# Gated-loop attention with a squared-ReLU block: the first unit's last pair of heads computed with steps on partitions and transposed on TensorE

## The chip, the cores and the metric

The kernel runs on one core of a Trainium2 chip. The metric is device time in microseconds. Three runs of the kernel before gave 648.28, 649.67 and 650.78; the median is 649.67.

## The reference

```
# q, k, v, a_re, a_im: (4, 8, 768, 48); w_in: (384, 2048); w_out: (2048, 384); all float32
mag = sqrt(a_re**2 + a_im**2)
scale = minimum(mag, 0.999) / (mag + 1e-6)
ar, ai = a_re * scale, a_im * scale
for t in range(768):                       # S_re, S_im: (4, 8, 48, 48), zero at the start
    S_re, S_im = ar_t * S_re - ai_t * S_im + outer(k_t, v_t),  ar_t * S_im + ai_t * S_re
    y_t = q_t @ S_re
x = y, heads side by side                  # (3072, 384)
out = maximum(x @ w_in, 0)**2 @ w_out      # (3072, 384)
```

So each head carries a complex state through 768 steps, and its rows of y, put side by side, go through two dense products.

## The kernel before

The 3072 rows are worked off in six units of 512 steps (NU = 6, L = 512), each in four chunks j of C = 128 steps (W = 4). The eight heads go in four pairs (NP = 4). The attention of a unit ends in xT, the transposed input of the dense part: xT[128 rows, unit % 2, m, 512 steps], where m is one of three blocks of 128 model columns. Pair i fills model columns 96 i to 96 i + 95: pair 0 and the first third of pair 1 lie in m=0, the rest of pair 1 and 64 columns of pair 2 in m=1, and the last 32 columns of pair 2 and all of pair 3 in m=2.

For a pair, these steps follow each other (lines of the kernel before):

- turn_pe transposes the scaled q and k on TensorE (L1660) and ACT copies them to QT (L1664).
- score makes the products of q and k (L1681, into bank sc0 or sc1, here sc_115 and sc_116), and DVE multiplies them by the causal mask into A (L1684).
- keep makes the chunk's contributions to the state (L1730, into tr_117 or tr_118), which ACT (L1740) or DVE (L1744) adds up in St and S.
- mix makes y of the pair: for unit 0, two products for each chunk and head, A with v (L1769) and the rotated q with the state St (L1773). The product's rows are the head's dimensions, two heads at partitions 0 to 47 and 64 to 111 of one bank. ACT copies the bank to the buffer yt (L1784), and DMAs bring its rows to their place in xT (L1797).

Unit 0's last pair (pair 3, heads 6 and 7) is done in two halves of 256 steps (by_half), the first in bank yp, the second in tr_118; its DMAs go half on SP's queue and half on ACT's. In the tables of order below, yt_94 and yt_95 are the two buffers yt (pair 2 has yt_94, pairs 1 and 3 yt_95), d_112 to d_114 the banks of the dense part, w_66 is the converted w_in and w_67 a buffer of w_out; aq_69 and f_70 belong to unit 1's inputs.

The dense part (function dense) multiplies w1 with xT (L1830, three matmuls for each block of 128 hidden columns and 256 steps, one for each m), applies ReLU and the square (L1863, L1864), and multiplies by w2 (L1878, or L1941 and L2086 in later units). For the first group of unit 0, six blocks have their m=0 and m=1 matmuls as twelve single steps ahead of everything else ("early" steps); the m=2 matmul of these blocks comes as a step of its own ("late").

On POOL, a small copy from xT's last rows of m=2 (the gate, L2179) stands ahead of the conversion and the fetches of later pieces of w_out. The conversion of the weights into the two-part form in which TensorE multiplies them (L978 to L992) runs on ACT and DVE between all this.

The order of the instructions on every engine is written out: the table ORDER gives for each engine a list of step numbers, and each engine's queue is filled in that order. SP and ACT issue DMAs in the same order.

Of the kernel before, what the change touches and what calls it, by code (L numbers as in the profile page):

```python
# [481 lines left out]
class Plan:  # L482
# [12 lines left out]
            220-222 2 0-1 5 4 224 3 6 225 223 226 14 7 13 15 9 17 16 8 228 19 12 11 18 10 20 227  # L495
            229 22 230 21 23-25 237 236 234 231 238 235 233 232 26-27 239-240 28 243 30-31 29 242
            241 35 49 33-34 42 32 48 46 45 47 43 244 44 246 245 40 36 38-39 37 41 51 50 55 57 54
            53 59 52 58 56 66 63 68 248 65 67 69 64 247 62 74 76 73 75 78 80 77 79 250 249 85 90
            60 84 89 87 91 88 86 61 72 71 70 81 83 82 93 92 252 254 253 251 99 95 101 94 98 96-97
            110 100 107 105 104 257 106 109 255 258 108 256 111 121 116 119-120 117-118 122 115  # L500
            261 260 262 259 132 130 133 131 129 103 127 126 128 102 112 123 114 113 124 135 125
            134 268 265 267 269 263-264 266 270 137-138 136 141 140 142 146 143 149 153 139 148
            152 272 150 271 147 151 160 159 162 157 163 161 164 158 273-274 173 171 169 175 174
            145 154 168 172 156 170 155 144 165 167 166 176-177 278 276 275 277 180 178 185 183
            182 181 184 192 194 190 179 188 193 189 191 195 204 206 202 205 201 200 203 199 186
            211 214 213 217 212 216 215 210 198 187 196-197 207 209 208 219 218 281 280 282 279
            283-285
        """,
        "POOL": """
            74-75 78 173 72 79 174 184 76 156 175 80 122 77 181 139 179 178 182 177 73 176 180 183  # L510
            9 8 10-11 13 12 14-15 89 185-186 189 188 187 82 17 91 83 81 84 191 86 85 90 95 0 19-20
            1 190 193 18 22 92 94 21 192 26 24 93 195 23 16 2 96 25 3 97 194 102 104 98 100 105 99
            103 101 27 109 108 28 30-31 34 29 33 112 32 41-42 87 107 111 38 106 37 36 110 39 35
            113 40 118 198 114 201 121 120 116 200 196 199 115 119 117 197 123 126 45 43-44 55 48
            127 46-47 125 129 52 51 53 128 130 124 50 88 54 49 137 134 132 204-205 4 133 5 203 138
            131 207 202 136 206 135 140 59 56 143 58 142 147 57 60 62-63 61 146 6 145 144 141 7
            213 152 211 155 148 154 149 210 151 150 212 153 159 208 64 164 67 65 160 66 209 68 158
            157 162 161 71 69-70 163 214 216 218 215 217 220 222 219 221 171 170 165 224 167 223
            172 169 168 226 225 227 166 230 228-229
        """,  # L520
        "PE": """
            539-553 0-1 554 2-3 555-559 4-6 560 7 561-565 8 566-570 42 571-574 44-45 43 48 53 51
            46-47 54 52 57 50 56 62 60 55 61 63 49 66 59 64 58 65 69-72 75 68 73 67 74 76 152
            77-79 154 160 155 161 153 162-163 158 166 156 164 159 165 167 172 157 174 173 168 178
            169 179 176-177 175 196 180 197 170 188 171 189-190 181-182 202-203 191 183 192
            184-185 193-194 186 195 187 200-201 198-199 206-207 204-205 212-213 210 208 80-81 209
            82 214 83 9 84-85 10 211 88 87 220 89-90 221 215 86 11-12 91-92 216 95 94 217 97 96
            222 98 14 13 99 218 223-225 93 15 102 101 100 219 226-227 103 16 228 232 229 231 233
            230 238-239 242 244 234-237 240 243 245 241 246-252 254 253 255-265 268-269 266-267
            270-273 17 105 104 276-278 274 279 275 106-107 18 108 281 280 282-284 111 110 109  # L530
            19-20 286 285 287-290 113-114 112 291-292 115 293-294 296 295 299 297-298 301-302 300
            303-304 307-308 305-306 309-312 314 313 315-316 319 317-318 320-321 323 322 324-326
            331-332 327-328 337 329-330 333 338 335-336 334 21 116-117 339-340 343 341-342 22 118
            23 120 119 345 344 347 346 25 123 122 121 24 349 348 350-352 26-27 124 126 125 355 353
            28 127 354 356-357 359 358 362-364 360-361 365 368 366-367 369-370 372 374 373 371 375
            377 376 378-382 386 383-385 387-391 394-396 392-393 400 397-398 401 399 29 128-129 402
            404 403 405 130 31 30 131-132 406-407 409 408 410 32-33 134-135 133 34 412 411 413 416
            414-415 136 35-36 138 137 418 417 139 419 422 420-421 427 423 425 428 424 426 433
            429-432 435-436 434 437-445 447 446 448-449 451-452 450 453-454 457 455 458-459 456
            463 460 464 461-462 465 469 466-468 38 140 37 141 471 473 143 142 39 144 470 472 475  # L540
            474 145 40 146-147 476 479 477 480 478 150 149 148 481 151 482 486 485 483 490 484 488
            487 492 489 491 496 493 498 497 494-495 499-500 505 501-502 506 503-504 509 508 511
            507 512 510 513 515 514 516-519 521 520 522-527 529 41 528 531 530 532-538
        """,
        "DVE": """
            363-364 367-368 365 371 366 372 369-370 375 377 376 378 373 381-382 374 383 379 384
            380 386 393 385 394 387 395-396 388 397-398 390 399-400 389 401-402 391 403-404 392
            510-511 405-426 428 427 429-430 432 431 433-434 436 435 437-440 442 441 443 486 444
            472 446 449-451 474 461 452 473 475 462-463 477 453 445 464 476 487-488 455 454 489
            456 447-448 457-458 478 459 465 491 466 490 467 460 468-470 480 479 471 481 186 492  # L550
            187 482 184-185 483 512 494 493 484 191 485 495 522 192 496-497 189-190 498 188 513
            499 519-520 194 196 500 197 195 514-515 193 521 523 198-201 524 202 526 525 516 528
            517-518 532 501 527 534 502 203 530 529 506 503 507 535 531 504 546-547 505 533 508
            548 509 549 558-559 550 560-561 551 562 552 563 553 564 555 565 554 566-567 556-557
            568-569 536 570-571 537 572 540 573-577 538 578 539 579-580 541 581-592 542 593 543
            594-595 544 596-598 545 600 599 601-602 607 604 608 603 609 605 610 606 617-618 615
            643 611 629-630 616 645 657 644 620 631 619 658-659 646 621 632 648 634 633 623 622
            647 624 660 625 635 626-628 636 661-662 637 649 638-639 612 640-642 206 663 651 650
            207 613-614 652 205 204 653 665 654 664 666 655 667-668 656 669-670 743 216 211 217
            210 208 224 209 744 218 745 749 228 750 746 671-672 212 673-674 213 676 675 747 677  # L560
            748 214 751 678 752 220 683-684 219 685 221 686 215 688 687 679 689-691 680 692 682
            681 694 693 696 695 697-705 223 706-715 225 716-717 227 718 226 719-724 229 725-729
            230 730-731 733 732 735 739 734 738 736 740 737 0 741 795 767 755 769 756 753-754 768
            1 757-758 3 2 4 770 797 742 772 7 759 5 9 6 8 771 783 761 773 760 762 10 763-764 796
            765 12 11 774 13 775 784 776 766 777-779 14 780 231-233 798 800 799 781-782 786 785
            239-240 801 241 787 803 802 804 236 805-806 235 234 237 788 238 789 222 790-791 807
            792-794 808 247-249 255 242 881 15 244 243 18 256-257 16 245 17 882 19 246 883 21 20
            251 22 887-888 250 809 260 24 261 23 884 810 252 811-813 253 814 262 815-816 254 885
            25 886 259 258 889 27 26 890 28 821-824 826 825 29 827-829 817-818 830 819 832 831 820
            833-855 30 856-870 876 871 891 877 872 878 873 892 874 879 875 894-896 33 897 31 898  # L570
            908 32 36 34 880 899 37 909 35 39 900 38 910-911 901 40 902 42 903 43 41 904-907 44
            263-265 913 912 271 914 272-273 916 915 917-918 266-267 919-921 45 279 268 280 269 46
            281 988 287-289 274 48 276-277 893 49 275 47 270 989 52 990 283 50 994 282 995 51 922
# [155 lines left out]
def fast_path(ctx, tc, q, k, v, a_re, a_im, moe_w_in, moe_w_out, out, flag):  # L729
# [874 lines left out]
    def pairs(n, which):  # L1604
# [197 lines left out]
        def by_half(i):  # L1802
            return n == 0 and i == NP - 1
# [447 lines left out]
```

## Time and profile before

| | |
|---|---|
| median of three runs | 649.67 us (648.28 to 650.78) |
| the profiled execution | 650.27 us |
| its span, first to last instruction | 648.1 us |
| mean granted TensorE clock | 0.985 |
| instructions | 12935 |

A row of a timeline reads: start in us, duration in us, engine, line, operation, output<-inputs, shape, and how many instructions are in it; brackets give the idle time ahead of it and what ended it. Durations of matmuls in a row overlap, because they are pipelined; the distance of starts tells the rate. A matmul in float32 shows as two passes ("x2"). The windows' rows give for each stretch the busy time of each engine; the chain is the work that ended last, followed back from the end. Starts are counted from the span's begin.

### The profile page before, as it was taken

The numbers are of one execution on the slowest core, as the hardware profiler recorded it, in microseconds if no ns is written. First come the engines' busy times: TensorE is split into PE (matmuls) and PEld (weight loads), VectorE is DVE, ScalarE is ACT, GpSimd is POOL, SyncE is SP. The second block draws the span as 40 slices with busy tenths as digits, with TensorE's granted clock in tenths as the row PEclk, the third lists the DMA queues.
The fourth block names the chain that finished last, engine by engine and source line by source line (L and its number), as shares of the span: only waits on it lengthen the run. The fifth ranks groups of instructions, "written<-read, shape, count | busy, mean of one in ns | idle before, by whom it ended". The sixth has DMA issues, their size and how long they took to land.

```text
span 648.1 us, 12935 instructions
## 1 busy us (share of the span) xinstructions
PE 603.7 (93%) x4762; PEld 539.9 (83%) x4762; DVE 581.9 (90%) x1192; ACT 378.9 (58%) x760; POOL 149.7 (23%) x266
## 2 busy tenths in 40 slices
PE   0448999999999999999999999999999999999995
PEld 0337987687778989999989999989989989988995
DVE  7999999999999999999988999988999998479981
ACT  7269998788868547536556636466545553432530
POOL 7401110145130034032123041113031042025200
PEclk9968999999999999999999999999999999999999
DMA  6973585026640057452076563066350064369721
GB/s 220 336 222 82 120 226 162 8 58 166 166 108 13 6 108 181 123 146 52 7 156 157 115 143 61 13 165 166 86 144 23 16 144 112 80 217 299 252 74 31
DMA packets 55913, 80.42 MB, mean 124 GB/s; under 512 B 12032, under 2 KB 38400, under 8 KB 55840
## 3 DMA queue, kind: packets, MB, share of 16 engines
q0 software_dynamic: 16064, 42.12, 23.6%
q1 hardware_dynamic: 35168, 31.93, 19.8%
q10 hardware_dynamic: 4608, 5.44, 3.2%
q8 instruction: 40, 0.66, 0.5%
q14 instruction: 33, 0.27, 0.1%
HBM read 48.76 MB, written 4.72 MB: 83 GB/s over the span
## 4 chain that ended last, share of the span: by engine, by line
PE 86%; DVE 6%; DMA 2%; ACT 1%; issue 1%; SPq 1%; ACTq 0%; DVEq 0%
PE d L1830 30%; PE d L1941 27%; PE d L1878 6%; PE sc L1681 5%; PE tr L1730 3%; PE yp L1762 3%; PE d L2086 2%; PE yp L1765 2%; PE tr L2086 2%; PE sc L1830 2%; PE sc L2086 1%; DMA xT<-yt 1%; PE d L1660 1%; DVE f L1150 1%; PE tr L1660 1%; PE yp L2086 1%
## 5 line engine op out<-in xcount | busy, mean ns | idle before, releaser
L1830 PE MATMUL d<-xT,w 128*128 128x256 f32 x888 | 197.9, 380 | 1.0 <-DMA xT<-yt 1.0
L1830 PEld LDWEIGHTS d<-xT,w 128*128 128x128 f32 x888 | 167.7, 190 | 25.1 <-issue 2.0
L1941 PE MATMUL d<-T,g 128*128 128x192 f32 x576 | 100.6, 328 | 0.3 <-DVE g L1957 0.3
L1941 PEld LDWEIGHTS d<-T,g 128*128 128x128 f32 x576 | 94.0, 190 | 1.5 <-DVE g L1957 0.6
L1896 POOL DMA_DIRECT2D out_dram<-ot x80 | 48.5, 610 | 157.8 <-DVE ot L1966 140.0
L1863 ACT ACTIVATE g<-d 128x512 f32<-128x512 f32 x74 | 43.7, 591 | 63.0 <-PE d L1830 55.3
L1941 PE MATMUL d<-w,g 128*128 128x192 f32 x432 | 76.7, 328 | 0.0
L1941 PEld LDWEIGHTS d<-w,g 128*128 128x128 f32 x432 | 71.0, 190 | 1.3 <-ACT g L1864 0.2
L1582 POOL DMA_DIRECT2D KC<-f x60 | 36.0, 604 | 127.5 <-DVE f L1545 120.0
L1864 ACT ACTIVATE g<-g 128x512 f32<-128x512 f32 x80 | 50.5, 631 | 2.5
L1957 DVE TENSOR_TENSOR g<-g 128x512 f32<-128x512 f32 x72 | 48.4, 682 | 3.9 <-PE d L1941 3.6
L1480 DVE TENSOR_TENSOR f<-aq,xn 128x384 f32<-128x384 f32 (+1 forms) x72 | 45.9, 682 | 0.0
L1634 DVE STREAM_TRANSPOSE aq<-f 128x384 f32<-128x384 f32 (+1 forms) x51 | 44.0, 910 | 0.2
L1878 PE MATMUL d<-w,g 128*128 128x384 f32 x128 | 43.7, 489 | 0.0
L1681 PE MATMUL sc<-QT 96*64 96x64 f32 (+1 forms) x736 | 38.6, 250 | 0.0
L1150 DVE TENSOR_TENSOR f<-aq 128x384 f32<-128x384 f32 x72 | 36.8, 550 | 0.2
L1681 PEld LDWEIGHTS sc<-QT 96*64 96x64 f32 x736 | 35.1, 137 | 2.0 <-issue 1.4
L1966 DVE TENSOR_TENSOR ot<-ot,d 128x192 f32<-128x192 f32 x70 | 23.6, 347 | 14.4 <-PE d L1941 14.0
L1878 PEld LDWEIGHTS d<-w,g 128*128 128x128 f32 x128 | 23.7, 190 | 14.0
L1073 POOL DMA_DIRECT2D v<-in_v_dram x30 | 23.3, 778 | 34.4 <-ACT junk L1452 25.7
L1511 ACT ACTIVATE f<-aq 128x768 f32<-128x768 f32 (+1 forms) x16 | 17.3, 1080 | 14.9 <-DVE aq L1497 14.9
L1730 PEld LDWEIGHTS tr<-v,KC 128*33 128x33 f32 (+1 forms) x544 | 19.2, 126 | 4.3 <-issue 3.4
(329 smaller groups left out, 1169.4 us busy)
## 6 DMA issues: line engine op xcount, KB each, us to landing
QT<-aq SPq DMA_DIRECT2D x136, 64.0 KB, 2.2
f<-in_moe_w_in_dram POOLq DMA_DIRECT2D x8, 768.0 KB, 6.7
f<-in_moe_w_out_dram POOLq DMA_DIRECT2D x8, 768.0 KB, 5.1
QT<-aq ACTq DMA_DIRECT2D x68, 64.0 KB, 2.2
KC<-f POOLq DMA_DIRECT2D x40, 96.0 KB, 3.1
out_dram<-ot POOLq DMA_DIRECT2D x80, 48.0 KB, 3.6
xT<-yt SPq DMA_DIRECT2D x34, 96.0 KB, 2.3
T<-in_moe_w_out_dram POOLq DMA_DIRECT2D x4, 768.0 KB, 7.8
```

Of the source, the lines that this page charges most:

```text
L1150: lambda c=c, j=j: dve.tensor_tensor(out=f[:, j], in0=a[:, :, :, c - 1], in1=a[:, j, :, c].unsqueeze(1).to_broadcast([C, 2, HH, D]), op=AL ...
L1480: lambda j=j, r=r: dve.tensor_tensor(out=f4[:, j, r], in0=a[:, r], in1=over(j), op=ALU.mult), rk)
L1634: lambda src=src, dst=dst: dve.transpose(out=dst, in_=src), rank)
L1681: pe.matmul(sa[p0:p0 + CH, j, t0:], lhsT=T[:, j, 1, h, t0:t0 + CH], rhs=T[:, j, 0, h, t0:], start=True, stop=True)
L1830: pe.matmul(ps, lhsT=w1[:, f // FP, m, ts(f % FP, C)], rhs=xT[:, n % 2, m, ts(grp, G)], start=(m == 0), stop=(m == NM - 1))
L1863: act.activation(out=o, in_=ps, func=AF.Relu)
L1864: act.activation(out=o, in_=o, func=AF.Square)
L1878: pe.matmul(ps, lhsT=gt[:, f % 2, ts(i, C)], rhs=w2[:, f], start=(f == 0), stop=(f == NF - 1))
L1896: dma(pool, [("ot", o, 0), ("ot", o, 1)], [], lambda p0=p0: pool.dma_start(out=out[r + p0:r + p0 + QC, :].rearrange("(t c) e -> c t e", c= ...
L1941: pe.matmul(bank[b][:, 0:DH], lhsT=gsets[x][h][:, j - HW * h, r], rhs=w(j), start=first and j == 0, stop=last and j == NT - 1)
L1957: lambda: dve.tensor_tensor(out=g[:, :, o], in0=g[:, :, x0], in1=g[:, :, x1], op=op),
L2086: pe.matmul(ps[:, jj], lhsT=u[:, ts(jj, C)], rhs=v_, start=i == 0, stop=i == len(terms) - 1)
```

## The change

In unit 0, pair 3 is computed the other way round. The product's rows are now the 128 steps of a chunk and its columns the 48 dimensions of a head (A and QT are the weights, v and the state the moving side). ACT copies a half (two chunks, two heads) to yt, whose first 32 columns of each chunk POOL has set to zero; TensorE transposes each chunk of 128 x 128 into a free part of the same bank; and ACT (upper 64 rows) and DVE (32 rows) copy that to xT. The two copies and four DMAs of before go. A key x5 stands for the part of xT that DVE writes. The table ORDER is replaced as a whole, on all five engines; of it only the effects shown below are told. Line numbers behind this place are 41 higher, those of the score and the state 3 higher: L1830 becomes L1871, L1684 L1687, L1744 L1747, L1797 L1838.

```diff
     def xk(n, ms, gs=(0, 1)):
-        return [("xT", n % 2, m, g) for m in ms for g in gs]
+        return ([("xT", n % 2, m, g) for m in ms for g in gs]
+                + [("x5", g) for m in ms for g in gs if n == 0 and m == NM - 1])
...
             y = take("yt", 2)
+            if by_half(i):
+                lead = C - 2 * D
+                step("POOL", 0.4, [], [("yt", y, 0), ("yt", y, 1)], lambda: pool.memset(
+                    yts[y].rearrange("p (j c) -> p j c", c=C)[:, :, 0:lead], 0.0), rank)
             for js, gs in ((range(2), [0]), (range(2, W), [1])) if by_half(i) else ((range(W), [0, 1]),):
...
+                if by_half(i):
+                    flat = bank[b][:, 0:len(js) * 2 * D].rearrange("p (j h d) -> p j h d", h=2, d=D)
+                    side = bank[b][:, L - C * len(js):L]
+                    def steps_first(js=js, flat=flat):
+                        for j in js:
+                            for h in range(2):
+                                o = flat[:, j - js[0], h]
+                                pe.matmul(o, lhsT=aa[h][:, j], rhs=v5[:, j, 2 * i + h],
+                                          start=True, stop=at[j] is None)
+                                if at[j] is not None:
+                                    pe.matmul(o, lhsT=T[:, j, 0, h], rhs=at[j][:, h],
+                                              start=False, stop=True)
+                    def as_rows(js=js, side=side):
+                        for q, j in enumerate(js):
+                            pe.transpose(side[:, ts(q, C)], yts[y][:, ts(j, C)], ident)
...
+                    step("PE", 0.45 * len(js), ..., [(b,)], steps_first, rank)
+                    step("ACT", ..., act.copy(
+                             out=yts[y][:, cols].rearrange("p (j c) -> p j c", c=C)[:, :, lead:],
+                             in_=flat.rearrange("p j h d -> p j (h d)")), rank)
+                    step("PE", 0.11 * len(js), yg, [(b,)], as_rows, rank)
+                    step("ACT", ..., act.copy(
+                             out=xT[64:C, n % 2, NM - 1, cols], in_=side[64:C]), rank)
+                    step("DVE", ..., dve.tensor_copy(
+                             out=xT[lead:64, n % 2, NM - 1, cols], in_=side[lead:64]), rank)
+                    continue
```

TensorE, from the end of pair 3's product to the dense stream (a row of 128x256 without a count is one early or late step). Before:

```order
L1769 MATMUL tr_118<-A_91,v_78 48x128
L1773 MATMUL tr_118<-QT_75,St_93 48x128 x2
L1830 MATMUL d_114<-xT,w_66 128x256
L1830 MATMUL sc_116<-xT,w_66 128x256
L1830 MATMUL d_114<-xT,w_66 128x256
L1830 MATMUL sc_116<-xT,w_66 128x256
L1830 MATMUL d_113<-xT,w_66 128x256
L1830 MATMUL yp<-xT,w_66 128x256 x2
L1830 MATMUL sc_115<-xT,w_66 128x256
L1830 MATMUL d_114<-xT,w_66 128x256
L1830 MATMUL d_112<-xT,w_66 128x256
```

The first two of these steps read m=0, and the third row of 128x256 (d_114's second) is the first that reads m=1; the next d_114 after sc_115 is the first late one, on m=2. One early step stood ahead of the product. After:

```order
L1773 MATMUL tr_118<-v_78,A_91 128x48
L1776 MATMUL tr_118<-St_93,QT_75 128x48
L1871 MATMUL sc_115<-xT,w_66 128x256
L1871 MATMUL d_114<-xT,w_66 128x256
L1871 MATMUL sc_116<-xT,w_66 128x256
L1781 MATMUL yp<-ident,yt_95 128x128 x2
L1781 MATMUL tr_118<-ident,yt_95 128x128 x2
L1871 MATMUL d_112<-xT,w_66 128x256
L1871 MATMUL sc_116<-xT,w_66 128x256 x5
L1871 MATMUL d_112<-xT,w_66 128x256
```

Three early steps now stand ahead of the product, three between it and the transposes, and two (d_112 and the first of sc_116's five) between these and the first late step, which is the second of the five.

DVE, from the masks of pair 3 on. Before:

```order
L992 ISA w_66<-w_67,w_66 128x1536 x2
L1744 TENSOR_TENSOR S_89<-tr_118,St_92 96x96
L1684 TENSOR_TENSOR A_90<-sc_115,mask 128x512
L1684 TENSOR_TENSOR A_91<-sc_116,mask 128x512
L1744 TENSOR_TENSOR St_93<-tr_118,St_93 96x96
L985 TENSOR_SCALAR w_66<-w_67 128x768
L1744 TENSOR_TENSOR St_93<-tr_118,St_93 96x96
L985 TENSOR_SCALAR w_66<-xT 128x768
```

After:

```order
L1687 TENSOR_TENSOR A_91<-sc_116,mask 128x512
L988 TENSOR_SCALAR w_66<-w_67 128x768
L1747 TENSOR_TENSOR St_93<-tr_118,St_93 96x96
L995 ISA w_66<-w_67,w_66 128x1536
L992 SCALAR_TENSOR_TENSOR w_66<-g,w_66 128x768
L995 ISA w_66<-g,w_66 128x1536
L995 ISA w_66<-T,w_66 128x1536
L1796 COPY xT<-yp 32x256
L1796 COPY xT<-tr_118 32x256
```

Four conversions of w_in now stand between the pair's last state and DVE's copies into xT.

SP's queue in unit 1, whose pair 1 is in yt_95 first, then pair 2 in yt_94, then pair 3 in yt_95 again. Before:

```order
L1797 DMA xT<-yt_94 16x512
L1797 DMA xT<-yt_95 32x512
L1797 DMA xT<-yt_95 48x512
L1797 DMA xT<-yt_94 48x512
L1797 DMA xT<-yt_95 16x512
L1797 DMA xT<-yt_94 32x512
L1797 DMA xT<-yt_95 48x512 x2
```

After:

```order
L1838 DMA xT<-yt_95 16x512
L1838 DMA xT<-yt_95 32x512
L1838 DMA xT<-yt_95 48x512
L1838 DMA xT<-yt_94 32x512
L1838 DMA xT<-yt_94 16x512
L1838 DMA xT<-yt_94 48x512
L1838 DMA xT<-yt_95 48x512 x2
```

Pair 1's three transfers now stand ahead of all of pair 2's. In unit 0 the last transfers of pair 2 likewise stand together now, without the load of aq_69 that stood between two of them.

More of the change, by code (lines that the diff above doesn't have):

```diff
@@ new lines @@
+            89 88 87 85 83 86 58 84 69 68 70 80 79 81 90-91 249 251 250 252 98 93 92 96 94-95 97
+            108 104 103 107 99 102 106 253 109 105 254-256 116 113 115 117-120 114 257-260 131 127
+            125-126 129 128 130 101 124 112 100 122 111 110 121 123 132-133 268 266 264 262-263
+            265 267 261 134 140 138 141 137 147 150 136 148-149 139 135 151 145-146 269-270 144
+            161 155 162 158 157 159 156 160 271-272 142 166 153 169 171-172 168 173 167 170 143
+            152 154 165 163-164 174-175 273-274 276 275 179 177 182 176 189 186 180 191 183 193
@@ new lines @@
+            169 167 165 176 172 180-181 177-179 182 198 190-191 199 173 183 204 184 192 205 193
+            185-187 194-197 188-189 202-203 200-201 210 208-209 211 206-207 214-215 82-83 212
+            84-85 216 86 10 9 87 222 89-90 223 217 91-92 218 11 88 93 12 94 219 97 220 96 224
+            98-99 213 225-226 13 101 100 14 95 227 15 104 103 102 221 228-229 16 105 234 230-231
+            233 235-236 238 232 242 240 246 237 239 241 244-245 243 250 248-249 251 247 253 252
+            255 254 256 258 257 260 259 262 261 263-269 272-273 270 274-275 278 271 279 17 107 18
@@ new lines @@
+            106 276 280-281 277 108 282 284 109 19 110 283 285-287 113 111-112 20 288 290-291 289
+            292-293 115-116 114 294 117 295 298 297 296 299 301 300 303 302 305 304 307 306
+            308-309 311 310 312-318 321 319-320 322 325 323-324 326-329 331 330 332-334 337 335
+            338-339 336 340 21 119 118 341-345 23 122 120-121 22 347 346 348-350 24-25 124-125 123
+            26-27 353 355 351-352 354 126-128 357 356 129 28 358 361 359-360 364-365 362-363
+            366-368 370-371 369 372-379 381 380 382 384 383 385-388 390 389 391-392 394 393
@@ new lines @@
+            396-397 395 398 402 399-400 403 401 30 131 130 29 404 406 405 407-408 132 31 134 133
+            409 411 410 412 33 137 136 32 135 413 416 414 417 415 418 138 35 140 34 139 419-420 36
+            141 421-422 424 423 425-429 431-432 430 433-434 437-438 435 439 436 440 442 441 443
+            445 444 447 446 449-451 448 452-453 455-456 454 459-462 457-458 465-466 463-464
+            467-468 471 469-470 38 37 142-143 475 473 144 146 145 39 472 474 476 147 40 148-149
+            477 479 481 478 480 150 152 151 482-483 153 484 488 492 487 485-486 489-490 494 491
@@ L544 @@
+            493 495-496 502 499 501 497 500 498 507-508 506 503-504 511 514 509-510 512-513 515
+            505 516-519 521 520 523 522 524-527 529 528 531 41 532 530 533 537 535 538 536 534
+            539-540
         """,
         "DVE": """
[L546 to L548 removed]
@@ new lines @@
+            457 456 491 458 480 459-460 467 492-493 468 461-462 469 494 470-471 481 472-473 514
+            482 186 483 187 484-485 184-185 496 495 191 497 486-487 188 518 192 498 528 499 189
+            521 190 500 196 501 197 515 193 530 516 195 194 522 198 523-524 517 199 502 201 200
+            526 202 525 519-520 531 204-205 527 503 505 504 534 508 535 509 506 548-549 536 532
+            550 533 529 507 551 510 552 511 553 560-561 538 562 554-555 563 557 564-565 556 566
+            558 567 569 568 537 571 570 559 572-573 540 574-577 539 578-579 541 580 542 581-582
@@ new lines @@
+            543 583 203 584-585 544 586-591 546 592 545 593-594 547 595-600 602 601 604 603 610
+            605-606 609 607 611 608 612 617 619-620 618 631 633 622 621 614 632 634 623 613 636
+            635 647-648 624-625 645 615 626 616 637 627-628 661 646 659 226 629 638 630 639 660
+            640 649-650 662 641-642 651 643 663-664 644 208 206 665 209 207 653 666 652 667 654
+            668 655 669-670 656-657 671-672 658 745 218 213 210 212 211 219-220 746-747 751-752
+            673-676 748 677 216 230 215 678 214 749 679 750 680 753 222-223 754 221 685 217 686
@@ new lines @@
+            278 49 277 279 50 272 47 52 291 991 280 51 992 286 996 287 54 285 53 997 924-925 288
+            926-927 929 284 928 993 930 294 931 295 932 55 933 292 934 293 994 56 995 57 998 58
+            999 936-937 59 938-945 935 946-966 296 967-976 978 977 980 979 60 982 981 986 985 983
+            987 984 988 1005 1003-1004 63 1006 61 1007-1008 989 64 1000 62 1009 66-67 65 68-69
+            1017 1010-1011 70 1012 72 71 1013 1001 1014 73 1015 74 1016 297-299 304 1019 1002 305
+            1018 1020 306 1021-1023 75 1025 1024 301 1026 302 300 1027-1030 311-313 308 303 307
@@ new lines @@
+            309 76 318 1103 78 319 79-80 77 315 314 320 81-82 1104 310 83-84 1105 1109-1110 316
+            1031 85 1106 1032 86-87 1033-1034 323 1035 322 321 1107 317 1036 1108 1111-1112 88
+            1043 89 1044-1046 1037-1038 1040 1048 1047 1049 1039 1050 1042 1051 1041 1052 1054
+            1053 1056 1055 1057-1087 90 1088-1091 324 1093 1092 1095 1094 1098 1096-1097 1113 1099
+            93 91-92 1100 94 1101 1127 97 96 95 1115 98-99 1116 1114 1102 1129 1118 100 1117 102
+            101 1128 1119 103 1130-1132 1121 1120 104 1122-1124 1133 1125-1126 325-327 333-335
@@ new lines @@
+            1135 1134 1136 105-106 1137-1139 330 338 331 328-329 332 339 1140 341-343 337 336
+            108-109 340 107 112 357 349 358 110 350-351 360 354-355 114 111 356 346 345 113 344
+            347-348 359 120 115 361 353 117 352 116 121 119 124 118 122-123 125-127 364 128 1143
+            132 362 1144 129-130 1145 133 131 363 1141 134 1142 1151 1146 139 135 1147 136 141
+            1148 140 138 1149-1150 137 153 1153 1152 1154 142 1155 146 1156 143-144 147 1157 148
+            1159 1158 149 1160 1163 150 1164 154 156 145 155 157 151 159-160 1161 1165 158 162
@@ new lines @@
+            377 389 387 390 99 382 611 208 101 612 607 613 385 614 608 384 383 102 397 396 398 394
+            100 386 399 615 393 105 392 391 616 103-104 617-618 395 619 403 400-402 404 209-210
+            107 106 211 621 620 109 108 212 110-111 213-214 625 119 215-216 609 626 623 622 217
+            112 405 113-114 406 408 218 628 118 220 407 409 219 115 221 116-117 418 222 630 415
+            120 412 624 413 416 410 417 223 411 122 224 633 424 225 125 123 425 427 414 419 421
+            121 426 420 422 124 629 634-636 428 226 431 127 429 637 423 435-436 433 126 638 434
@@ new lines @@
+            430 639 631 128 640 642 641 129 432 438 440 437 439 627 441 227-228 643 230 229 131
+            130 645 231 133 135 132 134 136 646 650 138 644 137 233 232 234 648 235 147 632
+            139-140 649 141 236 142 238 146 239 143 237 446 445 455 144 241 240 443-444 452-453
+            243 454 442 242 145 450 447 449 448 461 451 464 462 456 150 457 463 244 459 458
+            148-149 473 152 460 472 151 471 470 467-468 466 465 469 474 476 475 477-478 245 250
+            248 255 247 252 251 647 246 254 260-261 256-257 262 265 249 258 253 259 263-264 266
@@ L1757, in mix @@
                 cols = slice(C * js[0], C * (js[-1] + 1))
+                if by_half(i):
[13 more added lines that the diff above has]
+                            pe.transpose(side[:, ts(q, C)], yts[y][:, ts(j, C)], ident)
+                    yg = [("yt", y, g) for g in gs]
+                    step("PE", 0.45 * len(js), [k for h in range(2) for k in AK[got["A", i, h]]]
+                         + [("v", vs(n)), ("QT", got["T", i], 0), ("QT", got["T", i], 1)]
+                         + [("S", n % 2, i)] * (0 in js) + [("st", s, j) for j in js if j],
+                         [(b,)], steps_first, rank)
+                    step("ACT", ac(2 * D * len(js)) + 0.05, [(b,)], yg,
+                         lambda flat=flat, cols=cols: act.copy(
+                             out=yts[y][:, cols].rearrange("p (j c) -> p j c", c=C)[:, :, lead:],
+                             in_=flat.rearrange("p j h d -> p j (h d)")), rank)
+                    step("PE", 0.11 * len(js), yg, [(b,)], as_rows, rank)
+                    step("ACT", ac(C * len(js)) + 0.05, [(b,)], [("xT", 0, NM - 1, g) for g in gs],
+                         lambda side=side, cols=cols: act.copy(
+                             out=xT[64:C, n % 2, NM - 1, cols], in_=side[64:C]), rank)
+                    step("DVE", tt(C * len(js)) + 0.1, [(b,)], [("x5", g) for g in gs],
+                         lambda side=side, cols=cols: dve.tensor_copy(
+                             out=xT[lead:64, n % 2, NM - 1, cols], in_=side[lead:64]), rank)
+                    continue
                 def go(js=js, ps=ps):
```

172 lines of the change are left out of this document (54 added, 118 removed).

## The prediction

> **What bounds the kernel now.** I read four views in this order: busy time, the span cut at the places where TensorE starts and stops, TensorE's waits, and the chain that ended last.
>
> ```profile
> PE 603.7 (93%) x4762; PEld 539.9 (83%) x4762; DVE 581.9 (90%) x1192; ACT 378.9 (58%) x760; POOL 149.7 (23%) x266
> ```
>
> The same by stages (window, length, then busy time and instructions of PE, PEld, DVE, ACT and POOL, the granted clock, the DMA share and GB/s):
>
> ```profile
> 0.00:57.69 57.69, 22.03 (x112) 17.68 (x113) 52.08 (x125) 35.36 (x72) 22.33 (x57) 0.88 0.73 225
> 57.69:85.49 27.80, 26.59 (x431) 23.63 (x431) 27.03 (x54) 25.54 (x44) 3.22 (x6) 0.94 0.54 128
> 85.49:641.43 555.94, 555.12 (x4220) 498.58 (x4220) 501.86 (x1013) 318.05 (x646) 124.14 (x203) 1.00 0.44 114
> 641.43:648.10 6.67, 0.00 (x0) 0.00 (x0) 0.97 (x3) 0.00 (x0) 0.00 (x0) 0.81 0.14 39
> ```
>
> From 85.49 to 641.43 TensorE works 555.12 of 555.94 us. The time is therefore: when the dense stream starts, plus TensorE's work, plus a fixed tail of 6.67. The change can win only in the first 85.49 us, or 0.8 behind them. It can lose anywhere it adds TensorE work or a wait.
>
> TensorE's waits over the whole span (engine, line, what it waited for: total, times, longest):
>
> ```profile
> PE d L1600 <- DVE aq L1130: 20.2, 1, 20.2
> PE tr L1184 <- DVE xn L1299: 12.1, 2, 11.2
> PE d L1660 <- DVE f L1545: 2.1, 1, 2.1
> PE d L1830 <- DMA xT<-yt: 1.0, 2, 0.7
> ```
>
> The first two lie before 52 us, on VectorE's work for the first unit, which the product's form doesn't touch. Only the fourth concerns xT: 0.7 once, 0.3 once. Which rows of xT were late? The chain and the timeline around it (start, length, what, and in brackets the idle time ahead with its releaser):
>
> ```profile
> 80.25 1.14 SPq L1797
> ...
> 81.44 0.61 SPq L1057
> ...
> 82.10 3.25 DMA xT<-yt
> ...
> 85.49 0.67 PE L1830 MATMUL d<-xT,w 128*128 128x256 f32 x2 [0.74 <-DMA xT<-yt]
> 86.86 1.03 PE L1830 MATMUL yp<-xT,w 128*128 128x256 f32 x4
> 87.72 0.59 PE L1830 MATMUL sc<-xT,w 128*128 128x256 f32 x2
> 86.78 0.28 POOL L2179 COPY gate<-xT 128x1 f32<-128x1 f32 x1 [15.54 <-DMA xT<-yt]
> ```
>
> SP issued the late transfer at 82.10, and it landed 3.25 later, at 85.35. The last pair's first copy out of PSUM starts later, at 82.85 (row below), so the transfer that held TensorE at 85.49 is that of pair 2 (its rows of block m=1), not the one the change takes away. The last pair's rows release the gate at 86.78. The order lists six early steps (blocks m=0 and m=1) from 85.49 on before the first that reads m=2, and the rows at 86.86 and 87.72 are steps of two passes at 0.43 each. That first late step so starts at 87.72 + 0.43 = 88.15, 1.37 after the gate. The DMA that the change removes is hidden.
>
> **The change part by part.** *Removed copies and DMAs.*
>
> ```profile
> 82.85 0.37 ACT L1784 COPY yt<-yp 112x256 f32<-112x256 f32 x1
> 84.38 0.53 ACTq L1797 DMA_DIRECT2D xT<-yt  x1
> ```
>
> Two such copies, two issues on ACT and two on SP go: worth 0, because of the 1.37 of slack. SP's later loads move up by two issues, but TensorE waits for no load behind 57.69.
>
> *The product.* 14 matmuls in f32, 28 passes, before and after. Before, a pass streams 128 steps against 48-wide weights and two heads run side by side; after, 48 columns stream against 128-wide weights. Rows for before, then the nearest for after:
>
> ```profile
> 82.57 0.45 PE L1769 MATMUL tr<-A,v 128*48 128x128 f32 x4
> 82.79 0.45 PE L1773 MATMUL tr<-QT,St 96*48 96x128 f32 x4
> 83.23 0.45 PE L1773 MATMUL tr<-QT,St 96*48 96x128 f32 x4
> 52.56 0.28 PE L1600 MATMUL d<-lv,ident 128*128 128x2 f32 x2
> 52.70 0.91 PE L1600 MATMUL d<-ident 128*128 128x128 f32 x6
> 54.14 1.06 PE L1600 MATMUL d<-ident 128*128 128x128 f32 x8
> 55.03 0.60 PE L1660 MATMUL d<-ident,f 128*96 128x128 f32 x4
> 52.67 0.75 PEld L1600 LDWEIGHTS d<-ident 128*128 128x128 f32 x6
> 80.48 0.67 PE L1730 MATMUL tr<-v,KC 128*64 128x48 f32 x16 [0.47 <-DVE S L1744]
> ```
>
> Before: four passes start 0.22 apart, 0.055 each, 28 x 0.055 = 1.54. After, three prices. Sixteen passes with 48 columns and 64-wide weights take 0.67, 0.042 each: a floor, with half the weights. Two passes of 2 columns against 128-wide weights start 0.14 before the next group: 0.07. Eight passes with 128-wide weights take from 54.14 to 55.03: 0.11, and six weight loads of that width take 0.75, 0.125 each. I take 0.11, from the longest run of equally wide weights: 28 x 0.11 = 3.08, +1.54. At 0.07 it is 1.96, +0.42; at 0.042, -0.36.
>
> *The transposes.* Four single passes of 128 columns by the rows at 54.14: 4 x 0.11 = +0.44. ACT's copies into yt stand ahead of them; three early steps (3 x 0.43) cover these copies (0.37 by ACT's row). Without that cover TensorE would wait some 0.5.
>
> *What VectorE and ScalarE now do for xT.* Two copies of 64x256 on ACT, 0.37 each by the row at 82.85, behind one activation of 0.84 (L1115, by the like row of L1108 below); two of 32x256 on DVE behind four conversions of w1. For DVE's list:
>
> ```profile
> 82.34 0.55 DVE L985 TENSOR_SCALAR w<-xT 128x768 uint32<-128x768 uint32 x1
> 82.81 0.95 DVE L992 CUSTOM_DVE_ANT_0 w<-w,w 128x1536 uint16<-128x1536 uint16 x1
> 83.68 0.55 DVE L985 TENSOR_SCALAR w<-g 128x768 uint32<-128x768 uint32 x1
> 62.98 0.69 DVE L1684 TENSOR_TENSOR A<-sc,mask 128x512 f32<-128x512 f32 x1 [0.66 <-PE sc L1681]
> ```
>
> Up to the last state of this pair the new order has three L985 more (0.47 by the starts 82.34 and 82.81) and one L992 less (0.87): +0.54. One L992 and one L1545 now stand ahead of the first mask, so the 0.66 that it waited at 62.98 goes. Net -0.1. Behind that state four conversions take 4 x 0.87 = 3.5, and DVE's copies begin at 86.3 to 87.3. ACT's are done near 87. xT is whole at about 87, as at 86.78 before, so the gate on POOL and the fetches behind it stay where they are.
>
> *TensorE's end of the stage.* Before, the last four passes started at 83.23, so the product ended at 83.23 + 4 x 0.055 = 83.45. After: 83.45 - 0.1 + 1.54 = 84.9. Pair 2's transfers now stand together in SP's list with no load between them (the row of 0.61 at 81.44 stood there), and two activations that stood ahead of pair 2's copy on ACT now stand behind it:
>
> ```profile
> 75.77 0.84 ACT L1108 ACTIVATE f<-f 128x768 f32<-128x768 f32 x1
> 77.46 0.85 ACT L1110 ACTIVATE f<-f 128x768 f32<-128x768 f32 x1
> ```
>
> So I let m=1 land some 1.4 us earlier (an estimate from these two, less what overlaps at their ends), near 84, and the 0.74 goes. Three early steps, 86.2; transposes, 86.65; two early steps, 87.5: eight early steps done, xT whole. Before, the same eight ended at 85.49 + 5 x 0.43 = 87.65. Net -0.15; at 0.07 a pass, -1.0 with xT just in time (ends: -1.27 with no wait at all, +0.3 if m=1 still lands at 85.35).
>
> *Unit 1.* The new list of SP puts pair 1's transfers ahead of pair 2's.
>
> ```profile
> 189.02 0.59 ACT L1784 COPY yt<-yp 112x512 f32<-112x512 f32 x1 [3.70 <-DMA xT<-yt]
> 189.06 0.67 PE L1830 MATMUL d<-xT,w 128*128 128x256 f32 x2 [0.29 <-DMA xT<-yt]
> ```
>
> ACT there waited 3.70 for a buffer whose transfer stood behind another's. That goes, with TensorE's 0.29: -0.3. Everything else that is re-ordered behind 85.49 runs beside a busy TensorE: 0.
>
> *Sum.* -0.15 - 0.3 = -0.45 against the profiled execution's own 650.27 (its span 648.1 and 2.17 around it): 649.8. The median of the runs, 649.67, stands 0.6 below that, so 649.2; at 0.07, 648.3.
>
> **The rivals.** *The clock (either sign).*
>
> ```profile
> 55.63:57.69 2.06, 0.00 (x1) 0.03 (x1) 2.06 (x5) 2.02 (x4) 0.00 (x0) 1.00 0.48 119
> 57.69:58.40 0.71, 0.71 (x7) 0.71 (x8) 0.71 (x2) 0.69 (x4) 0.00 (x0) 1.00 0.00 0
> 58.40:61.80 3.40, 3.40 (x36) 2.90 (x33) 3.37 (x10) 2.68 (x6) 1.07 (x2) 0.52 0.49 105
> ```
>
> TensorE idled 2.06 us waiting for DVE, and 0.7 later ran 3.4 us at half clock: 1.7 us lost. The new order splits that gap: I make it some 1.6 us ahead of the first transposes, 2.1 between the K side and the q side, and 1 before pair 1. If a second stretch of 3.4 is lost, +1.7: 650.9; with two, +3.4: 652.6, slower by 0.45%. It decides where DVE's chain leaves TensorE idle over 2 us within one such stretch. Against it: each gap is shorter than the old one or equal. If instead no stretch is lost, -1.7: 647.5, and at 0.07 a pass 646.6. The Trainium skill, "TensorE: Matmul & The Clock Gate", section "What's actually happening", gives a free-running window of 3413 ns and halves the clock after an idle one; the length agrees with 3.40, the condition doesn't, since 2.06 us idle sufficed here. By its rule neither order would lose such a stretch behind 44.75, and the new one would have -1.7 from this, as in the case just priced.
>
> *xT late (slower side).* DVE's copies behind four conversions: if DVE runs 2 us later than I place it, they end at 89.5 and TensorE stands at 87.5 with only xT's m=2 steps next: +2, and the gate on POOL, later by as much, delays w_out's fetches, +1 to +2 more: 652 to 653.5. For it: DVE is 97% busy there (27.03 of 27.80). Against: nothing new stands in its list but 0.54. It decides from 87.5 on.
>
> *Nothing moves*: the wait at 85.49 is merely replaced by the added passes and unit 1's stays: 649.7. It lies inside the forecast's own range of 648 to 650.3.
>
> **How the numbers follow.** Forecast, with the neutral rival in it, 0.55 (649.2). Clock kept or passes at 0.07 with it, 0.20 (646.6 to 647.8). More half clock, 0.15 (650.9 to 652.6). xT late, 0.10 (652 to 653.5). Leaving out the last tenth above and half of the gain's best end below gives 646.5 to 652.2. A change of 0.5%, 3.2 us, is about what a measurement of this kernel tells from none: below 646.4 lies the clock's gain with its best end (0.13), above 652.9 the second half-clock pair and half of the late case (0.10).
>
> **What would show it.** Right: L1773's passes 0.11 apart; no wait of TensorE on xT in unit 0; the gate at 86 to 88; no 3.70 on ACT in unit 1; one stretch of half clock near 60. Wrong: a wait of L1871 on DVE's or ACT's copy into xT, two such stretches, or idle time of TensorE behind 90 us.

## The result, and the profile after

The changed kernel took 654.08 us (median of nine runs, 651.83 to 655.27), the kernel before 649.57 beside it: a ratio of 1.0064, 95% interval 1.0050 to 1.0079. It is slower by 4.2 us, between 3.2 and 5.1. The prediction was 649.2, with a range of 646.5 to 652.2 and a chance of 0.10 for slower by more than 0.5%: the time lies above the range, on the side that it gave least.

The first part of the page of the kernel after:

```profile
PE 608.2 (93%) x4766; PEld 542.7 (83%) x4766; DVE 582.0 (89%) x1194; ACT 378.7 (58%) x762; POOL 151.3 (23%) x267
```

Its windows, cut where the half clock starts and ends, where the eighth early step ends (89.35) and where TensorE ends:

```profile
57.95:64.70 6.75, 6.15 (x47) 4.83 (x47) 5.64 (x13) 5.12 (x12) 1.08 (x2) 0.50 0.48 119
64.70:89.35 24.65, 24.65 (x396) 22.75 (x392) 22.45 (x43) 22.64 (x38) 2.74 (x5) 1.00 0.55 132
89.35:645.80 556.45, 554.35 (x4211) 496.19 (x4210) 501.01 (x1011) 317.46 (x646) 124.56 (x203) 1.00 0.43 113
645.80:652.50 6.70, 0.00 (x0) 0.00 (x0) 0.97 (x3) 0.00 (x0) 0.00 (x0) 0.69 0.19 52
```

The kernel before, from the end of its eighth early step to the end of TensorE:

```profile
87.65:641.43 553.78, 552.96 (x4212) 496.65 (x4210) 499.73 (x1010) 315.89 (x645) 123.56 (x202) 1.00 0.44 114
```

The spans differ by 4.4 (648.1 and 652.5). Up to the eighth early step the new kernel is 1.70 later, behind it another 2.67 (556.45 against 553.78), and the tail is the same. Of the 2.67, 1.28 is idle time of TensorE (2.10 against 0.82), and 1.39 is as many passes keeping it busy for longer (554.35 against 552.96). The granted clock is half for 6.75 us instead of 3.40: two stretches in place of one.

The product, the transposes, and the first step that reads m=2 (of the ten passes at 88.92 the first two are the eighth early step, the next two the first late one); then the gate and the copies into xT:

```profile
84.23 0.39 PE L1776 MATMUL yp<-St,QT 96*128 96x48 f32 x2
84.45 0.39 PE L1773 MATMUL yp<-v,A 128*128 128x48 f32 x2
...
88.05 0.38 PE L1781 MATMUL yp<-ident,yt 128*128 128x128 f32 x2
88.27 0.38 PE L1781 MATMUL tr<-ident,yt 128*128 128x128 f32 x2
88.49 0.60 PE L1871 MATMUL d<-xT,w 128*128 128x256 f32 x2
88.92 2.48 PE L1871 MATMUL sc<-xT,w 128*128 128x256 f32 x10
...
88.54 0.42 DVE L1796 COPY xT<-yp 32x256 f32<-32x256 f32 x1 [0.93 <-PE yp L1781]
88.99 0.37 ACT L1793 COPY xT<-yp 64x256 f32<-64x256 f32 x1 [0.73 <-DVE xT L1796]
89.66 0.42 DVE L1796 COPY xT<-tr 32x256 f32<-32x256 f32 x1 [0.71 <-ACT xT L1793]
90.14 0.97 POOL L2220 COPY gate<-xT 128x1 f32<-128x1 f32 x1 [5.44 <-DVE xT L1796]
```

Two passes of the product start 0.22 apart, and so do two transposes: 0.11 each, as taken. TensorE waits for nothing here. But DVE and ACT take turns (DVE, ACT twice, DVE), each waiting for the other by about 0.7, so xT is whole at 90.08, 1.6 us behind the last transpose, and the gate opens 3.4 us later than before. Not all of that is the turns: the transposes themselves come late, behind the longer half clock.

TensorE's waits over the whole span, those behind the first unit:

```profile
PE d L1871 <- DMA xT<-yt: 1.1, 1, 1.1
PE sc L1684 <- DMA QT<-aq: 0.6, 2, 0.4
```

Both are at places where the kernel before had no wait. The first is in unit 3. Its place in the timeline of TensorE:

```profile
378.81 1.57 PE L1982 MATMUL d<-T,g 128*128 128x192 f32 x8
380.22 2.75 PE L1871 MATMUL d<-xT,w 128*128 128x256 f32 x12
384.06 2.18 PE L1871 MATMUL d<-xT,w 128*128 128x256 f32 x9 [1.09 <-DMA xT<-yt]
```

And in the chain (start, length, what):

```profile
378.72 0.59 ACT yt L1825
379.31 0.02 issue
379.33 0.52 SPq L1838
379.85 0.04 issue
379.89 4.04 DMA xT<-yt
```

The last pair's y leaves at 379.33 and lands at 383.93. Between its mix and the first step that needs it TensorE has 8 passes of the second product and 12 of the first; in the old order there were 16 of the second product, and no wait.

### The profile page after: what moved, and what is told of

It is laid out like the page before. It is cut to its first block, busy times and chain, and to the rows that moved or that the text cites. A ratio compares the mean times of both kernels' runs of the same rounds, so it can differ in the third digit from the quotient of the medians.

```text
span 652.5 us, 12917 instructions
## 1 busy us (share of the span) xinstructions
PE 608.2 (93%) x4766; PEld 542.7 (83%) x4766; DVE 582.0 (89%) x1194; ACT 378.7 (58%) x762; POOL 151.3 (23%) x267
## 4 chain that ended last, share of the span: by engine, by line
PE 79%; DVE 11%; DMA 5%; SPq 2%; issue 2%; ACT 1%; ACTq 0%; DVEq 0%
PE d L1871 27%; PE d L1982 25%; PE d L1919 6%; PE sc L1684 5%; PE tr L1733 3%; PE yp L1803 3%; SPq L1642 2%; DMA f<-in_moe_w_in_dram 2%; PE yp L1806 2%; PE sc L1871 2%; DVE f L1483 1%; PE d L1663 1%; DMA aq<-in_a_im_dram 1%; PE tr L2127 1%; DVE f L1548 1%
## 5 line engine op out<-in xcount | busy, mean ns | idle before, releaser
L1871 PE MATMUL d<-xT,w 128*128 128x256 f32 x888 | 197.4, 380 | 1.1 <-DMA xT<-yt 1.1
L1871 PEld LDWEIGHTS d<-xT,w 128*128 128x128 f32 x888 | 167.8, 190 | 24.9 <-issue 1.5
L1684 PE MATMUL sc<-QT 96*64 96x64 f32 (+1 forms) x736 | 39.9, 251 | 0.8 <-DMA QT<-aq 0.6
L1684 PEld LDWEIGHTS sc<-QT 96*64 96x64 f32 x736 | 35.7, 137 | 3.2 <-issue 2.1
L1687 DVE TENSOR_TENSOR A<-sc,mask 128x512 f32<-128x512 f32 x28 | 18.8, 682 | 5.0 <-PE sc L1684 4.9
```

The source lines that it names most:

```text
L1684: pe.matmul(sa[p0:p0 + CH, j, t0:], lhsT=T[:, j, 1, h, t0:t0 + CH], rhs=T[:, j, 0, h, t0:], start=True, stop=True)
L1871: pe.matmul(ps, lhsT=w1[:, f // FP, m, ts(f % FP, C)], rhs=xT[:, n % 2, m, ts(grp, G)], start=(m == 0), stop=(m == NM - 1))
```

## The experiments

The kernel before was timed beside each of them on the same chip, and each ratio is to that. The edits are shown in outline. The first three split the change: form without order, order without form. Profiles are of one execution each; where a difference between two of them is given, it can hold something of the run-to-run spread, which is 2.5 us for the kernel before.

**x1_form: the old order, the new form.** DVE's list had been given these two copies behind the wrong state (the third of the pair instead of the second), 15 places later than the expectation says.

```diff
 # old ORDER; steps_first and the copies to yt stand where the old product and copies stood
+PE:   ... four early steps, as_rows(yp), as_rows(tr_118), early steps ...
+ACT:  yt(yp), yt(tr_118), L983, xT(yp), xT(tr_118)
+DVE:  the two copies into xT, 6 places behind the pair's last state
-SP, ACT: the four DMAs
```

> The order of before on all engines, with only the form of unit 0's last pair changed (steps on partitions, transposes, copies by ACT and DVE into xT; the transposes stand behind four early steps, DVE's copies behind the second custom conversion of that stage). Theory 'order' (the re-planned order loses the time): the form adds 28 passes at 0.056 more each, 1.55, and four transposes, 0.44, and saves the 0.74 of waiting on xT and some of the 0.47 on the state: +0.8 against before, about 650.4. Rival 'form' (the new product path loses it): +2.5 to +4, 652 to 653.5.

Measured: 660.18, 1.0150 (1.0128 to 1.0172).

```profile
96.34 0.42 DVE L1818 COPY xT<-yp 32x256 f32<-32x256 f32 x1
96.90 2.05 PE L1894 MATMUL yp<-xT,w 128*128 128x256 f32 x4 [8.04 <-DVE xT L1818]
```

That is no verdict on the form: TensorE stood for 8.04 us because bank yp was not free until DVE's copy. It does price DVE's place in this list.

**x1b_form: the same, with the copies where they were meant.**

> As x1_form, with DVE's two copies into xT 15 places earlier in DVE's list, right behind the second custom conversion of the stage, near 87 us. Theory 'order': no long wait of TensorE on xT, and the form costs what it adds on TensorE less the two waits that it covers: +0.8 against before. If the 9.8 of x1_form came from the form and not from the place of the copies: 655 or more.

Measured: 650.20, 1.0005 (0.9988 to 1.0022). Beside the kernel before, the form by itself costs nothing that can be told (x8_form_fill, below, prices it otherwise). Behind 58.4 us TensorE waits there only once:

```profile
PE tr L1754 <- DVE S L1768: 0.6, 1, 0.6
```

**x2_order: the new order, the old form.**

```diff
 # new ORDER; old product where steps_first stands, old copies and ACT's DMAs behind each other
-PE: as_rows   -DVE: two copies into xT   -POOL: memset
+SP: the two DMAs, right behind pair 2's
+PE: two early steps moved behind the product
```

> The order of after on all engines, with the form of before for unit 0's last pair (products of two heads side by side, four DMAs into xT; two early steps moved behind the product so that the DMAs have the time they had). Theory 'order': +2.5 to +4 against before, 652 to 653.5, with two stretches of 3.4 us at half clock between 57 and 65 us and a wait of about 1 us on xT near 384 us. Rival 'form': within 1 us of before, 649 to 650.6.

Measured: 653.91, 1.0055 (1.0036 to 1.0074). So the order holds most of the loss, though 0.9 us of this kernel's time is a wait that after doesn't have. The expectation was wrong on the clock: this execution has one stretch of half clock (about 59.3 to 62.7), as the kernel before had, and is still 3.7 longer by its span. Its waits:

```profile
PE d L1860 <- DMA xT<-yt: 0.9, 1, 0.9
PE d L1860 <- ACT g L1895: 0.9, 1, 0.9
PE sc L1706 <- DMA QT<-aq: 0.6, 1, 0.6
```

The one on ACT near 98 us belongs to this kernel alone; the other two are after's.

**x3_after_fill and x4_before_fill: empty work in the gaps ahead of the half clock.**

```diff
+for x in range(12):      # x4: 10, all in the gap of 2.06
+    pe.matmul(bank["tr0"][:, 0:C], lhsT=ident, rhs=ident, start=True, stop=True)
```

> After, with 9 and 3 empty f32 matmuls (128x128, 0.22 each) in TensorE's gaps of 1.93 and 0.60 us at 55 to 59 us; nothing waits for their result. If the half clock from 58.0 to 64.7 us came from these gaps and costs what it seems: one or two stretches less, -1.4 to -2.8 against after, 651.3 to 652.7, and a clock of 0.984 to 0.987. If the clock there doesn't depend on the gaps, or the time isn't lost to it: as after, 654.1 within 0.5.

> Before, with 10 empty f32 matmuls in TensorE's gap of 2.06 us at 55.6 to 57.7. If the half clock from 58.4 to 61.8 came from this gap: -1.5 to -1.7, about 648.0, and no such stretch in the profile. If not: 649.6, with the stretch, within 0.4.

Measured: x4_before_fill 648.59, 0.9972 (0.9959 to 0.9986), as expected; x3_after_fill 654.48, 1.0064 (1.0041 to 1.0087), no gain, although its runs had a mean granted clock of 0.985 against after's 0.983. The windows of x4_before_fill (the granted clock is third from the end) where the gap and the stretch had been:

```profile
55.60:58.20 2.60, 2.60 (x25) 2.60 (x24) 2.60 (x7) 2.56 (x5) 0.00 (x0) 1.00 0.56 127
58.20:62.00 3.80, 3.80 (x64) 3.38 (x64) 3.77 (x9) 3.73 (x10) 1.08 (x2) 1.00 0.39 80
```

In x3_after_fill the stretches near 60 went too, but one came back at 86.9, behind two new waits:

```profile
80.59 1.10 PE L1899 MATMUL d<-xT,w 128*128 128x256 f32 x4 [0.45 <-DMA xT<-yt]
82.72 0.43 PE L1756 MATMUL tr<-v,KC 128*64 128x48 f32 x8 [0.60 <-ACT St L1766]
```

The window of the stretch, with the granted clock third from the end:

```profile
86.85:90.27 3.42, 3.42 (x12) 2.79 (x11) 1.35 (x3) 1.31 (x5) 0.00 (x0) 0.52 1.09 212
```

**x6_state_fill, x7_unit3, x9_all: single places of the new order mended.** x6_state_fill takes the second of those waits away: the new order has two conversions ahead of that state on ACT. x7_unit3 gives unit 3 the cover that it lacks, and x9_all is both.

```diff
 # x6, on ACT, with x3's fills
+  COPY St_93          # pair 3's first state
   ACTIVATE w_67, ACTIVATE g
-  COPY St_93
 # x7, on TensorE, unit 3
-  L1982 x8            # ahead of pair 3's mix
   mix(3)
+  L1982 x8
```

> x3_after_fill with one more edit: on ACT the copy of pair 3's first state stands ahead of two weight conversions (0.81 and 0.76 by the chain of x3_after_fill) instead of behind them. Theory 'two limits in the first 90 us' (TensorE at half clock and, as late, ACT's conversions ahead of that state): with both taken away the product of pair 3 starts 1 to 1.5 us earlier, and the time is 0.8 to 1.6 below after, 652.3 to 653.3 (ratio to before 1.004 to 1.0055). Rival: the first 90 us don't matter, as in x3_after_fill: 1.0064 within 0.001.

> After, with four f32 matmuls of the second product (8 passes, 1.4 us) moved in unit 3 from just ahead of pair 3's mix to just behind it, as before has 16 such passes there and after has 8. Theory: the wait of 1.09 on xT near 384 goes and the time falls by 0.8 to 1.1 (ratio 1.0047 to 1.0052). Rival: the wait is paid elsewhere (the mask or yt is late, or unit 3's attention is bound by SP): no change, 1.0064, with the wait turned into another near 377.

> After with the edits of x6_state_fill and x7_unit3 together. If the losses are separate and add: 1.8 to 2.6 below after, ratio 1.0025 to 1.0037; what is left is then the stalls from 520 to 610 us (1.8 more than before by my count). If they don't add: 1.005 or more.

Measured: x6_state_fill 652.57, 1.0057 (1.0037 to 1.0078); x7_unit3 653.46, 1.0062 (1.0041 to 1.0083); x9_all 652.72, 1.0044 (1.0025 to 1.0062). Neither mend alone can be told from nothing; both together may win back a third, but the interval of x9_all still meets after's. x7_unit3 is the most telling, because its profiled execution happened to have no half clock in the first unit:

```profile
57.95:64.70 6.75, 5.81 (x113) 4.92 (x112) 6.75 (x15) 6.70 (x13) 1.67 (x4) 1.00 0.48 119
64.70:87.24 22.54, 22.54 (x331) 20.41 (x327) 21.13 (x42) 20.74 (x37) 2.12 (x4) 1.00 0.59 138
87.24:645.30 558.06, 555.32 (x4211) 496.59 (x4210) 500.65 (x1011) 317.28 (x646) 125.08 (x203) 1.00 0.43 113
```

With the new order of the first unit, the eighth early step ends at 87.24, 0.4 ahead of the kernel before. Yet the rest takes 558.06, 4.3 more than before, and the whole span 652.1. The wait near 384 is gone, and these are there (after had the first too, with 0.6):

```profile
PE sc L1710 <- DMA QT<-aq: 0.8, 2, 0.5
PE tr L1759 <- DVE St L1773: 0.8, 1, 0.8
PE sc L2160 <- DVE aq L2172: 0.4, 1, 0.4
PE yp L1829 <- ACT QT L1722: 0.4, 1, 0.4
```

What TensorE won in the first unit isn't seen at the end. The six profiles with the new order behind this point (after, x2_order, x3_after_fill, x6_state_fill, x7_unit3, x9_all) say the same: the eighth early step ends anywhere between 87.3 and 90.9, and TensorE between 644.0 and 645.8. That it meets other engines in units 1 to 3 and hands the time back there is what the waits suggest; of the 4.3, though, they are only 1.9, and 2.4 is again longer busy time (555.32 against 552.96).

**h1_early to h4_untillast: the orders joined at a point.** All with the new form.

```diff
+head = steps of order X ahead of the cut
+line = [n for n in X if n in head] + [n for n in Y if n not in head]   # on each engine
```

> New form of unit 0's last pair; after's order on all engines until unit 1's first state (near 152 us), from there the order of before (as in x1b_form). Theory 'late waits' (the loss is small stalls in units 3 and 5): close to x1b_form, +0.3 to +1.2 against before, with the clock's second stretch in some executions. Rival 'start' (the loss is in the first 90 us, by the clock and the later products): +2.5 to +3.5.

> The mirror of h1_early: the order of before (with the new form) until unit 1's first state, then after's order. Theory 'late waits': +2.5 to +3.3 against before, with TensorE's waits of about 1.1 on xT near 384 and 0.4 on QT near 563. Rival 'start': within 1.

> New form; the order of before until unit 5's first state (near 534 us), then after's. 'Late waits': +1.2 to +2.0, since I count 1.8 more stalls from 520 to 610 us in after than in before. If those only pay back what units before them left over: within 0.6.

> New form; after's order until unit 5's first state, then that of before. What after loses is the sum of this and h3_last if the two add up: +2.3 to +3.0 here (0.8 to 1.7 in the first 90 us, 1.1 at 384). Rival: +4 or more, if the last unit's order has no part in it.

Measured: h1_early 1.0047 (1.0032 to 1.0061), h2_late 1.0076 (1.0053 to 1.0099), h3_last 1.0027 (1.0013 to 1.0041), h4_untillast 1.0069 (1.0045 to 1.0093). The pieces don't add: h1_early and h2_late give 8 us together where after loses 4.2. A joint has a price of its own, since the queues stand at different places of their lists there: h1_early waits 1.3 on DVE and h2_late 1.4 on ACT near the cut. Each mirror speaks for another theory: by h1_early alone, 3.1 us above before, the loss would lie at the start, and by h2_late, 4.9 above, in the late part. What h2_late shows in spite of its joint: the late part alone can lose as much as all of after, without after's first 150 us. On the last unit the two don't agree either: h3_last is above before, but its interval overlaps x1b_form's, and h4_untillast loses as much as after without that unit's order.

**m1_sp_before and m2_sp_after: SP's list exchanged.**

```diff
-line = order of after
+line = {e: before[e] if e == "SP" else after[e] for e in engines}      # m2: the reverse
```

> After on TensorE, DVE, ACT and POOL, with the order of before on SP's queue alone (the queue that brings y into xT and the transposed q and k into QT; the two orders agree in all dependencies, so this needs no other change). Theory 'SP': after's late waits of TensorE are on transfers of SP's queue (xT near 384, QT near 341 and 563), so its order makes them: 1.5 to 3 below after, ratio to before 1.002 to 1.004. Rival 'compute engines' (the transfers are late because what they carry is made late): 1.0064 within 0.0015, with the same waits.

> The mirror: the order of before on TensorE, DVE, ACT and POOL (with the new form, as x1b_form), after's order on SP's queue alone. Theory 'SP': 1.5 to 3 above x1b_form, ratio to before 1.003 to 1.005. Rival 'compute engines': as x1b_form, 1.0005 within 0.0015.

Measured: 657.92, 1.0132 (1.0108 to 1.0156), and 659.74, 1.0159 (1.0136 to 1.0182). Both theories fail: each list of SP is worth 4 us or more with the compute lists that it was planned with. An exchange can't tell which list is the better one, since each fits only its own partners. In m2_sp_after, TensorE's wait on transposed q and k rises to

```profile
PE sc L1864 <- DMA QT<-aq: 5.5, 3, 3.2
```

**x8_form_fill: the old order, the new form and x4's empty matmuls.**

> A version meant to beat both: the order of before, the new form (as x1b_form), and the 10 empty matmuls of x4_before_fill. If both add up: as x1b_form less 1.5 to 1.8, 647.8 to 648.7 beside a before of 650 (ratio 0.9965 to 0.998). If the form's added passes count fully once the clock is held: x4_before_fill plus 0.8, ratio 0.9985.

Measured: 650.88, 1.0024 (1.0007 to 1.0041). It keeps the full clock in its profile and still doesn't gain. It differs from x4_before_fill by the form alone, and the two lie 0.0052 apart, 3.4 us, with intervals that don't meet (they ran on different chips, each beside its own kernel before). So x1b_form's 1.0005 doesn't prove the form free: it costs 0.3 us by that run, 0.6 by after against x2_order, and 3.4 here. The order's price is steadier: 3.8 by after against x1b_form, 3.6 by x2_order against before, 2.6 by x3_after_fill against x8_form_fill. x4_before_fill, the kernel before with ten empty matmuls, beats both kernels, and nothing else does. Why the fills gain with the old form and not with the new stays open.

## Why the prediction was wrong

*The removed copies and DMAs, worth 0.* Not contradicted: x1b_form takes them out, with all the rest of the form, at 1.0005. The term alone was not tried, and with the fills the form costs more (x8_form_fill).

*The product and the transposes.* Right, 0.11 for a pass of either, as taken.

*xT whole at 87, the gate as before.* Wrong by 3.1 and 3.4 us. Two things add up to that. The transposes came 1.85 later than in my working (88.05 instead of 86.2), for the most part by the half clock. And I priced the four copies by their lengths and overlooked that the two engines wait for each other. x7_unit3, at full clock, shows the second without the first:

```profile
88.03 0.97 POOL L2253 COPY gate<-xT 128x1 f32<-128x1 f32 x1 [4.92 <-DVE xT L1822]
```

There the gate is 1.25 later than before, not 3.4. TensorE didn't wait for xT in unit 0 in either. What the later fetches of w_out cost was not tried by itself; x7_unit3, with the earlier gate, is no faster (1.0062).

*The eighth early step at 87.5.* In after's own profiled execution it was 89.35, with two stretches of half clock; in x7_unit3, with none, 87.24. The working stood on a profile with one stretch, and the clock's rival priced each at 1.7: that makes 89.2 with two, and 85.8 with none. The first comes out and the second doesn't, so the agreement is partly luck: the two stretches cost this step 2.1 (89.35 less 87.24), some 1.05 each and not 1.7. By that estimate, from two executions, 1.05 of the 1.70 is the stretch more, and 0.65 is the new stage itself, which I had put at -0.15. Nor is the clock the cause of most of the loss. In nine runs of after the mean granted clock was 0.9828, in 90 runs of the kernel before 0.9848: 0.002 of 652 us is 1.3 us at most, and x2_order's profile loses 3.7 by its span with no more half clock than before. The one run of after with a clock of 0.987 took 651.83, still 2.3 above the median before.

*Unit 1's wait of 3.70 on ACT and 0.29 on TensorE goes.* Right; the copy there now waits for TensorE:

```profile
190.17 0.59 ACT L1825 COPY yt<-yp 112x512 f32<-112x512 f32 x1 [2.54 <-PE yp L1806]
```

*"Everything else that is re-ordered behind 85.49 runs beside a busy TensorE: 0."* This is the step that failed: the term was put at nothing, from a row that didn't bear it. It measured +2.67 in after and +4.3 in x7_unit3. Counted from the seventeenth pass of the first product, where the eighth early step ends, to the last pass of TensorE, the stretch lasts 551.5 to 553.7 us in the four profiles with the old order in it (before, x1b_form, x4_before_fill, x8_form_fill), and 554.9 to 558.1 in the six with the new one. The ranges don't meet. The row of 555.12 busy of 555.94 showed that the old order left TensorE idle there for 0.82, and I read it as room. It leaves nearly nothing to win by fewer waits, and says nothing of what another order does. That one loses in two ways: idle time (0.0 to 1.1 in those four, 1.1 to 2.9 in the six), and busy time for as many passes (551.5 to 552.9, and 553.8 to 555.4). The first is waits on engines and transfers whose lists fit less well; DVE, 90% busy in this stretch (501.86 of 555.94), leaves little slack, but that this makes the waits was not shown. What makes the passes longer isn't shown at all; the granted clock reads 1.00 in both. One old-order profile has no idle time:

```profile
88.81:640.31 551.50, 551.50 (x4211) 496.89 (x4209) 500.78 (x1010) 316.71 (x645) 124.23 (x203) 1.00 0.43 113
```

That is x1b_form. I gave the loss no rival of its own: both rivals on the slower side lay in the first unit.

Where in units 1 to 5 the order loses is only partly settled. The waits on xT and QT in units 3 and 5 are seen; mending the first moves it on (x7_unit3), and exchanging SP's list alone does not mend it (m1_sp_before, m2_sp_after). I found no single place that holds it, and the cause inside the order stays open.

## What to carry to other kernels

Where a change re-plans every queue, cost the new order over the whole span, not at the edited place: a bound engine that is 99.9% busy says that the old order fits there, and an unknown new one deserves a range that opens mainly to the slower side. Time gained at the start can be gone by the end, as in x7_unit3. A busy share doesn't show all: half of the loss here was busy time for the same number of passes. And when two engines fill one tile from one bank, look at whether they wait for each other before adding up their lengths.

## What the runs showed of the hardware

The same gap of TensorE gave half clock or not from one execution to the next. In the kernel before, 2.06 us of idle were followed by 3.4 us at half clock; in x1b_form the same gap was followed by full clock (after and x7_unit3, alike up to unit 3, differ in the same way):

```profile
58.32 1.05 PE L1684 MATMUL d<-ident,f 128*96 128x128 f32 x8 [2.04 <-DVE f L1569]
```

```profile
59.00:62.40 3.40, 3.40 (x64) 2.98 (x64) 3.37 (x9) 3.35 (x8) 1.07 (x2) 1.00 0.48 103
```

And in x3_after_fill two gaps of 0.45 and 0.60 us, between 80 and 83, preceded 3.4 us at half clock from 86.9 on. The Trainium skill, "TensorE: Matmul & The Clock Gate", section "What's actually happening", has a window of 3413 ns that runs freely, independent of the kernel. That the same gap counts or doesn't, and the length of the stretch, agree with it. That it takes an idle window, as a table there has it, does not: none of these gaps was longer than 2.1 us. Ten empty matmuls of 0.22 us in such a gap were worth 1.8 us to the kernel before (x4_before_fill, 0.9 to 2.7), and nothing that showed to the kernels with the new form (x8_form_fill, x3_after_fill).
